# Shorter runs in the load of x, one last tile of 512 tokens, and GpSimd's share of layer 2 where it runs alone

## The chip, the cores and the metric

The kernel runs on 1 core of one Trainium2 chip. The metric is the device time of one execution in microseconds (us). Five engines work side by side, each through its own instruction queue in order: TensorE (PE, matmuls into PSUM), VectorE (DVE), ScalarE (ACT), GpSimd (POOL) and SyncE (SP, which here issues the DMAs).

## What is computed

```python
X = np.fft.fft(np.fft.fft(x, axis=1), axis=2).real        # x: 2 x 3008 x 256
x = X.reshape(6016, 256)
h = x @ w1_in; g = np.maximum(h, 0) ** 2; x = g @ w1_out  # layer 1: 256 -> 2048 -> 256
h = x @ w2_in                                             # layer 2: 256 -> 2048 -> 256
P = a[0] + a[1]*h + a[2]*h**2 + a[3]*h**3
Q = 1 + abs(b[0])*abs(h) + abs(b[1])*h**2
out = (P / (Q + 1e-6)) @ w2_out
```

Each operand of the large products is split into a rounded high part and a rest ("hi", "lo"), and a product takes three matmuls: hi hi, lo hi, hi lo.

## The kernel before

**Start.** x comes in nine loads (`x_load`, L231): one small one, then eight chunks of 4 units (the last of 3), each for 96 partitions. A chunk has four buffers (`xt`) to go to. `u_mm` (L238) multiplies a chunk with a 47-point Fourier matrix (L247), ACT copies one half of the result out of PSUM (`u_copy`) and DVE forms sums and differences (`u_out`, L263) into U. Loads of the weights (L315, L317) stand between those of x on SP's queue; ACT and DVE turn each weight block into fp32 hi and lo parts ("decode", L322 to L359). When all of U is there, small transforms (`f_d`, `f_s`, L473 to L503) give layer 1 its inputs, tile by tile; this is called F below.

**Tiles.** `TILES` counts units of 128 tokens: a first tile of 384 tokens, ten of 512, then two of 256. The hidden dimension is 16 chunks of 128. Layer 1 of a tile is, for each chunk, a product into `h` (`h1_mm`, L623 to L625; it works on half the columns of a tile, 256 for a tile of 512 and 128 for one of 256), ACT and DVE work, a low part on POOL (L694), and the product with `w1_out` (`mm_o`, L651). For a tile of 256 tokens two chunks share one bank of 512 columns. At the end of a tile ACT and DVE split the result in two (L700, L705).

**Layer 2** goes over sub-tiles of 256 tokens (`SUB`; 23 of them), each in eight groups of two chunks, that is of 512 columns. The last sub-tile has seven such groups and two single chunks (`SINGLES`). A group is a product into a bank `h2` (L592, 12 matmuls), then

- ACT: u = |scaled h| (L712), t1 (L717), w = |u| (L726), y (L739), z = y squared (L743)
- DVE: q (L722, into u's buffer), t2 (L730), t3 (L734), gh (L749), m (L755, into bank p3), e (L759)
- POOL: gl (L763), which also gives the low part its final form

and the product with `w2_out` (L651 with o2a as its output, 12 matmuls). t3 is the last reader of the bank h2, which is then given back.

**The order.** A planner (`Queues`, L62) simulates the engines with a cost for each operation (`act`, `dve`, `pool_tt`, `mm`), takes buffers and banks from named sets (`SLOTS`, `SPARE`) and writes out each engine's instruction order; a `place` settles which of several ready operations goes first. Layer 2 of a tile is placed one tile behind its layer 1 (L834): the PE does layer 1 of tile t among layer 2 of tile t - 1. So layer 2 of the last tile has no layer 1 beside it; it "runs alone".

Of the kernel before, what the change touches and what calls it, by code (L numbers as in the profile page):

```python
# [13 lines left out]
ALU = mybir.AluOpType  # L14
# [8 lines left out]
TILES = [3] + [4] * 10 + [2, 2]  # L23
# [16 lines left out]
LATE = (8, 5.18, 4.1, 3.03)  # L40
LAG_END = 4.67
POOLED = 2
# [114 lines left out]
def body(ctx: ExitStack, tc: tile.TileContext, x0, xf, w1i, w1o, w2i, w2o, a_in, b_in,  # L157
# [73 lines left out]
    def x_load(c):  # L231
        XT[c] = stp.tile([96, max(X_CH), 2, 256], F32, tag="xt", name="xt", bufs=SLOTS["xt"])
        if c == 0:
            nc.sync.dma_start(out=XT[c][:, 0:2], in_=x0)
        else:
            nc.sync.dma_start(out=XT[c][:, 0:XN[c]], in_=xf[:, S0[c] - 1:S0[c] - 1 + XN[c]])
# [39 lines left out]
    for c in range(NC):  # L276
        place = -32 + c
        n = XN[c]
        add(("x", c), "SP", 0.78 * n if c else 7.0, place, lambda c=c: x_load(c), take=("xt",), lat=X_LAT,
# [126 lines left out]
    for j, w in enumerate(wl):  # L406
# [4 lines left out]
        add(("wd", j), "SP", 2.1, place - 4, lambda j=j, w=w: w_load(j, *w), take=(raw,), lat=DMA_LAT,  # L411
# [37 lines left out]
    H1, H2, O1, O2 = {}, {}, {}, {}  # L449
    G1, G2, E1, E2, OB = {}, {}, {}, {}, {}  # L450
# [116 lines left out]
    def names(tag, t):  # L567
# [4 lines left out]
        if tag == "h2":  # L572
            return (BANKS5 if t else BANKS) + (SPARE["h2"] if t == M - 1 else ())
        return (tag,) + (SPARE1.get(tag, ()) if t <= 1 and tag == "g" else ()) + (SPARE.get(tag, ()) if t == M - 1 else ())
# [145 lines left out]
    def e2_q(t, j):  # L720
        w = E2[t, j]["w"]
        nc.vector.scalar_tensor_tensor(out=w, in0=w, scalar=b0, in1=H2[t, j], op0=ALU.add, op1=ALU.mult)  # L722
# [21 lines left out]

    def e2_gh(t, j):
        e = E2[t, j]
        x = sb(tag2("g2", t, j), [128, 2, NMAX], F32R)
        e["gh"], e["gl"] = x[:, 0, :e["n"]], x[:, 1, :e["n"]]
        nc.vector.scalar_tensor_tensor(out=e["gh"], in0=e["t1"], scalar=a0, in1=e["z"], op0=ALU.add, op1=ALU.mult)  # L749


    def e2_m(t, j):
        e = E2[t, j]
        e["m"] = ps(tag2("m", t, j), [128, NMAX])[:, :e["n"]]
        nc.vector.scalar_tensor_tensor(out=e["m"], in0=e["w"], scalar=Q1, in1=f32(e["gh"]), op0=ALU.add, op1=ALU.mult)  # L755

    def e2_e(t, j):
        e = E2[t, j]
        nc.vector.scalar_tensor_tensor(out=e["t1"], in0=e["t1"], scalar=a0, in1=e["m"], op0=ALU.add, op1=ALU.subtract)  # L759
# [73 lines left out]
    for t, (tile1, col, width) in enumerate(SUB):  # L833
        base = 16 * (tile1 + 1) + M2_AT + (LATE + (0,) * T)[tile1]  # L834
        for j, (first, gs) in enumerate(GROUPS2[t]):
# [14 lines left out]
            add(("q",) + key, "DVE", dve(n, ptr=1), place, f(e2_q), needs=[("u",) + key, ("t1",) + key])  # L850
            add(("t2",) + key, "DVE", dve(n), place, f(e2_t2), needs=[("t1",) + key])
            add(("t3",) + key, "DVE", dve(n, ptr=1), place, f(e2_t3), needs=[("t2",) + key], after=[("q",) + key],
                give=(given("h2", t, j),))
            add(("w",) + key, "ACT", act(n), place, f(e2_w), needs=[("q",) + key])
# [121 lines left out]
```

## Time and profile before

| | us |
|---|---|
| median of 3 runs | 1122.88 |
| lowest and highest | 1121.0, 1123.06 |
| the profiled execution's own time | 1124.36 |
| its span in the profile | 1122.5 |
| mean granted clock of TensorE | 0.985 |

The profile gives, for one execution, the busy time of each engine, single instructions in order of time, and what ended the idle time before them. In the rows below, "L651" is line 651 of the kernel, `o2a<-g,w2hi` an output and its inputs by tile name, and x12 a count of merged instructions. Times of instructions are counted from the span's start. An instruction's own time can overlap the next one's, so the distance between two starts is what it costs a full queue.

### The profile page before, as it was taken

Reading aid. Unit: us, or ns where it says so; the run is one execution under the profiler, and the core shown is the slowest. Engines: PE = TensorE matmul, PEld = TensorE weight load, DVE = VectorE, ACT = ScalarE, POOL = GpSimd, SP = SyncE. Lnnn points to the kernel's source line nnn. Section 1 sums busy time; section 2 is a strip of 40 time slices with the busy share of each in tenths; the row PEclk is TensorE's granted clock in tenths of the full one; section 3 lists DMA queues with packets and bytes.
Section 4 is the critical chain, followed back from the end, with each engine's and each line's share of the span. In section 5 each row is a group of like instructions: output and inputs, shape, how many; then the busy total and the mean of one; then the engine's idle time right before and its main releaser. Section 6 shows DMA issues by size and latency. Waiting matters only on the chain.

```text
span 1122.5 us, 21825 instructions
## 1 busy us (share of the span) xinstructions
PE 1086.1 (97%) x7932; PEld 1022.5 (91%) x7932; DVE 1027.2 (92%) x1821; ACT 982.0 (87%) x1995; POOL 472.4 (42%) x358
## 2 busy tenths in 40 slices
PE   7999998999999999999999999999999999999996
PEld 6889987989999999989999999999999999999995
DVE  3689999999999999999999899999999998999988
ACT  2378898999999989899999999999999999898884
POOL 0000004455455544455455454554454556354423
PEclk9889999999999999999999999999999999999997
DMA  8952510000000000000000000000000000000000
GB/s 215 258 203 76 172 45 1 1 25 10 1 20 11 1 20 10 1 20 11 1 20 10 2 20 11 3 18 10 1 15 11 6 10 11 11 1 11 11 10 10
DMA packets 25543, 36.68 MB, mean 33 GB/s; under 512 B 2203, under 2 KB 19229, under 8 KB 24765
## 3 DMA queue, kind: packets, MB, share of 16 engines
q1 hardware_dynamic: 25293, 35.17, 10.2%
q8 instruction: 63, 1.03, 0.4%
q14 instruction: 43, 0.35, 0.1%
q10 hardware_dynamic: 144, 0.13, 0.0%
HBM read 26.48 MB, written 8.78 MB: 31 GB/s over the span
## 4 chain that ended last, share of the span: by engine, by line
PE 64%; ACT 15%; DVE 13%; issue 4%; DMA 3%; SPq 1%; POOL 1%; DVEq 0%; ACTq 0%; POOLq 0%
PE o2a L651 16%; PE p L592 11%; PE o1a L651 8%; PE o1b L651 8%; PE p L623 6%; PE o2b L592 5%; DVE g L749 2%; DVE p L755 2%; ACT y L739 2%; ACT u L726 2%; DVE t L759 2%; PE p L605 2%; PE p L608 2%; ACT g L679 2%; ACT y L743 2%
## 5 line engine op out<-in xcount | busy, mean ns | idle before, releaser
L763 POOL TENSOR_TENSOR g<-t,y 128x512 fp32r<-128x512 f32 (+1 forms) x188 | 255.9, 1361 | 442.1 <-DVE t L759 343.4
L694 POOL TENSOR_TENSOR g<-g,g 128x512 fp32r<-128x512 f32 x160 | 214.0, 1338 | 187.6 <-ACT g L689 149.0
L651 PE MATMUL o2a<-g,w2hi 128*128 128x256 f32 (+1 forms) x1440 | 266.5, 287 | 8.6 <-POOL g L763 8.4
L651 PEld LDWEIGHTS o2a<-g,w2hi 128*128 128x128 f32 x1440 | 211.2, 191 | 19.4 <-POOL g L763 11.4
L749 DVE SCALAR_TENSOR_TENSOR g<-t,ab,y 128x512 fp32r<-128x512 f32 (+1 forms) x188 | 149.2, 796 | 13.4 <-ACT y L743 10.7
L651 PE MATMUL o2a<-g,w2lo 128*128 128x256 f32 (+1 forms) x720 | 146.1, 283 | 0.0
L651 PE MATMUL o1a<-g,w1hi 128*128 128x512 f32 (+1 forms) x384 | 144.8, 379 | 0.6 <-POOL g L694 0.5
L755 DVE SCALAR_TENSOR_TENSOR p<-u,g 128x512 f32<-128x512 f32 (+2 forms) x190 | 144.6, 761 | 0.8
L651 PE MATMUL o1b<-g,w1hi 128*128 128x512 f32 (+1 forms) x384 | 143.3, 375 | 0.0
L759 DVE SCALAR_TENSOR_TENSOR t<-t,ab,p 128x512 f32<-128x512 f32 (+2 forms) x190 | 138.3, 728 | 1.2
L726 ACT ACTIVATE u<-u 128x512 f32<-128x512 f32 (+2 forms) x190 | 118.1, 621 | 18.7 <-DVE u L722 17.8
L679 ACT ACTIVATE g<-g 128x512 f32<-128x512 f32 x160 | 100.9, 631 | 25.8 <-DVE g L669 24.7
L739 ACT ACTIVATE y<-u 128x512 f32<-128x512 f32 (+1 forms) x188 | 116.5, 621 | 4.9 <-POOL g L763 0.6
L743 ACT ACTIVATE y<-y 128x512 f32<-128x512 f32 (+1 forms) x189 | 117.0, 621 | 1.5
L722 DVE SCALAR_TENSOR_TENSOR u<-u,ab,p 128x512 f32<-128x512 f32 (+2 forms) x137 | 99.0, 723 | 18.7 <-ACT t L717 18.6
L592 PE MATMUL p<-x2h,w2hi 128*128 128x256 f32 (+1 forms) x520 | 106.9, 287 | 6.0 <-DVE t L734 4.0
L669 DVE TENSOR_TENSOR g<-p,bc 128x256 f32<-128x256 f32 x262 | 106.1, 418 | 7.1 <-POOL g L694 3.4
L651 PEld LDWEIGHTS o2a<-g,w2lo 128*128 128x128 f32 x720 | 111.8, 191 | 0.0
L685 ACT ACTIVATE g<-g 128x512 fp32r<-128x512 f32 (+1 forms) x175 | 109.4, 625 | 2.0 <-PE o1b L651 0.9
L689 ACT ACTIVATE g<-g 128x512 f32<-128x512 f32 (+1 forms) x175 | 109.2, 625 | 1.1
L592 PE MATMUL p<-x2l,w2hi 128*128 128x256 f32 (+1 forms) x520 | 105.5, 283 | 0.3 <-DVE x2l L705 0.2
L592 PE MATMUL p<-x2h,w2lo 128*128 128x256 f32 (+1 forms) x520 | 104.3, 282 | 0.0
(239 smaller groups left out, 2886.2 us busy)
## 6 DMA issues: line engine op xcount, KB each, us to landing
g<-in_dram SPq DMA_DIRECT2D x48, 256.0 KB, 3.1
xt<-in_dram SPq DMA_DIRECT2D x7, 768.0 KB, 10.2
out_dram<-os SPq DMA_DIRECT2D x21, 256.0 KB, 2.1
udram<-U SPq DMA_DIRECT2D x4, 640.0 KB, 5.1
ut<-udram SPq DMA_DIRECT2D x9, 256.0 KB, 3.0
x2h<-in_dram SPq DMA_DIRECT2D x8, 256.0 KB, 7.1
x2l<-in_dram SPq DMA_DIRECT2D x8, 256.0 KB, 5.2
xt<-in_dram SPq DMA_DIRECT2D x1, 576.0 KB, 8.8
```

The costliest lines, as they stand in the source:

```text
L592: nc.tensor.matmul(h[:, c * n:(c + 1) * n], l[:, k, :], r[:, k], start=(q == 0), stop=(q == 5))
L651: nc.tensor.matmul(O[t][e], l[:, e * 128:(e + 1) * 128], r[:, c * n:(c + 1) * n], start=(i == 0 and q == 0 and not one), stop=(i == NF - 1 ...
L679: nc.scalar.activation(out=e["g"], in_=e["g"], func=ACTF.Relu)
L685: nc.scalar.activation(out=e["gh"], in_=e["g"], func=ACTF.Square)
L694: eng.tensor_tensor(out=e["gl"], in0=e["g"], in1=f32(e["gh"]), op=ALU.subtract)
L726: nc.scalar.activation(out=w, in_=w, func=ACTF.Abs)
L739: nc.scalar.activation(out=e["z"], in_=e["w"], func=ACTF.Abs_reciprocal_sqrt, bias=Q1)
L743: nc.scalar.activation(out=z, in_=z, func=ACTF.Square)
L749: nc.vector.scalar_tensor_tensor(out=e["gh"], in0=e["t1"], scalar=a0, in1=e["z"], op0=ALU.add, op1=ALU.mult)
L755: nc.vector.scalar_tensor_tensor(out=e["m"], in0=e["w"], scalar=Q1, in1=f32(e["gh"]), op0=ALU.add, op1=ALU.mult)
L759: nc.vector.scalar_tensor_tensor(out=e["t1"], in0=e["t1"], scalar=a0, in1=e["m"], op0=ALU.add, op1=ALU.subtract)
L763: nc.gpsimd.tensor_tensor(out=e["gl"], in0=e["t1"], in1=e["z"], op=ALU.mult)
```

## The change

Four things are changed.

1. The host lays x out with the unit as the outer dimension, so that a chunk is read in runs of 2048 bytes for each partition and unit; before, each partition read one run of 8192 bytes.
2. `TILES` ends with one tile of four units in place of two of two units. The number of layer 2 sub-tiles stays 23; the last two now both belong to the last tile and run alone.
3. For 15 of the 17 groups that run alone (`ALONE`: all of both sub-tiles but the two single chunks), q is written into h's own bank, after t3; w and m stay in that bank; ACT adds a0 to t3's result (new operation P, `e2_p`); gh is a product on POOL and no longer a DVE operation; e becomes a plain subtraction on DVE. The bank is given back by e, u's buffer by q, and p3 is not used.
4. The planner's numbers: lower costs for the loads, layer 2 of the tile before the last is placed 1.5 places later (`BEHIND`), and the spare buffers and banks are open to both last sub-tiles.

```diff
-TILES = [3] + [4] * 10 + [2, 2]
+TILES = [3] + [4] * 11
...
-LATE = (8, 5.18, 4.1, 3.03)
+LATE, BEHIND = (8, 5.18, 4.1, 3.03), 1.5
...
+ALONE_FROM, ALONE_END = 0, 2
...
-            nc.sync.dma_start(out=XT[c][:, 0:XN[c]], in_=xf[:, S0[c] - 1:S0[c] - 1 + XN[c]])
+            nc.sync.dma_start(out=XT[c][:, 0:XN[c]], in_=xf[S0[c] - 1:S0[c] - 1 + XN[c]].rearrange("s p h d -> p s h d"))
...
-        add(("x", c), "SP", 0.78 * n if c else 7.0, place, lambda c=c: x_load(c), take=("xt",), lat=X_LAT,
+        add(("x", c), "SP", 0.55 * n if c else 7.0, place, lambda c=c: x_load(c), take=("xt",), lat=X_LAT,
...
-        add(("wd", j), "SP", 2.1, place - 4, lambda j=j, w=w: w_load(j, *w), take=(raw,), lat=DMA_LAT,
+        add(("wd", j), "SP", 1.5, place - 4, lambda j=j, w=w: w_load(j, *w), take=(raw,), lat=DMA_LAT,
...
+    ALONE = [(t, j) for t in (M - 2, M - 1) for j in range(len(GROUPS2[t]))][ALONE_FROM:-ALONE_END]
...
-            return (BANKS5 if t else BANKS) + (SPARE["h2"] if t == M - 1 else ())
-        return (tag,) + (SPARE1.get(tag, ()) if t <= 1 and tag == "g" else ()) + (SPARE.get(tag, ()) if t == M - 1 else ())
+            return (BANKS5 if t else BANKS) + (SPARE["h2"] if t >= M - 2 else ())
+        return (tag,) + (SPARE1.get(tag, ()) if t <= 1 and tag == "g" else ()) + (SPARE.get(tag, ()) if t >= M - 2 else ())
...
     def e2_q(t, j):
-        w = E2[t, j]["w"]
-        nc.vector.scalar_tensor_tensor(out=w, in0=w, scalar=b0, in1=H2[t, j], op0=ALU.add, op1=ALU.mult)
+        e, w = E2[t, j], E2[t, j]["w"]
+        e["w"] = H2[t, j] if (t, j) in ALONE else w
+        nc.vector.scalar_tensor_tensor(out=e["w"], in0=w, scalar=b0, in1=H2[t, j], op0=ALU.add, op1=ALU.mult)
...
+    def e2_p(t, j):
+        t1 = E2[t, j]["t1"]
+        nc.scalar.activation(out=t1, in_=t1, func=ACTF.Identity, bias=a0)
...
     def e2_gh(t, j):
...
+        if (t, j) in ALONE:
+            nc.gpsimd.tensor_tensor(out=e["gh"], in0=e["t1"], in1=e["z"], op=ALU.mult)
+            return
...
     def e2_m(t, j):
...
-        e["m"] = ps(tag2("m", t, j), [128, NMAX])[:, :e["n"]]
+        e["m"] = e["w"] if (t, j) in ALONE else ps(tag2("m", t, j), [128, NMAX])[:, :e["n"]]
...
     def e2_e(t, j):
...
+        if (t, j) in ALONE:
+            nc.vector.tensor_tensor(out=e["t1"], in0=e["t1"], in1=e["m"], op=ALU.subtract)
+            return
...
-        base = 16 * (tile1 + 1) + M2_AT + (LATE + (0,) * T)[tile1]
+        base = 16 * (tile1 + 1) + M2_AT + (LATE + (0,) * T)[tile1] + BEHIND * (tile1 == T - 2)
...
-            add(("q",) + key, "DVE", dve(n, ptr=1), place, f(e2_q), needs=[("u",) + key, ("t1",) + key])
+            alone = key in ALONE
+            free, held = (given("u", t, j),), (given("h2", t, j),)
+            add(("q",) + key, "DVE", dve(n, ptr=1), place, f(e2_q), needs=[("u",) + key, ("t1",) + key],
+                after=[("t3",) + key] if alone else [], give=free if alone else ())
...
-            add(("t3",) + key, "DVE", dve(n, ptr=1), place, f(e2_t3), needs=[("t2",) + key], after=[("q",) + key],
-                give=(given("h2", t, j),))
-            add(("w",) + key, "ACT", act(n), place, f(e2_w), needs=[("q",) + key])
-            add(("y",) + key, "ACT", act(n), place, f(e2_y), needs=[("w",) + key], take=(one_of("y", t, j),),
+            add(("t3",) + key, "DVE", dve(n, ptr=1), place, f(e2_t3), needs=[("t2",) + key],
+                after=[] if alone else [("q",) + key], give=() if alone else held)
+            add(("w",) + key, "ACT", act(n, alone), place, f(e2_w), needs=[("q",) + key])
+            add(("y",) + key, "ACT", act(n, alone), place, f(e2_y), needs=[("w",) + key], take=(one_of("y", t, j),),
...
-            add(("gh",) + key, "DVE", dve(n, ptr=1), place, f(e2_gh), needs=[("z",) + key, ("t3",) + key],
+            if alone:
+                add(("P",) + key, "ACT", act(n, ptr=1), place, f(e2_p), needs=[("t3",) + key])
+            gh = ("POOL", pool_tt(n)) if alone else ("DVE", dve(n, ptr=1))
+            add(("gh",) + key, *gh, place, f(e2_gh), needs=[("z",) + key, ("P" if alone else "t3",) + key],
...
-            add(("m",) + key, "DVE", dve(n), place, f(e2_m), needs=[("gh",) + key], port=True,
-                take=(one_of("m", t, j),), give=(given("u", t, j),))
-            add(("e",) + key, "DVE", dve(n, ptr=1), place, f(e2_e), needs=[("m",) + key], give=(given("m", t, j),))
+            add(("m",) + key, "DVE", dve(n), place, f(e2_m), needs=[("gh",) + key], port=not alone,
+                take=() if alone else (one_of("m", t, j),), give=() if alone else free)
+            add(("e",) + key, "DVE", dve(n, ptr=0 if alone else 1), place, f(e2_e), needs=[("m",) + key], give=held if alone else (given("m", t, j),))
...
-    xf, x0 = np.zeros((96, 31, 2, D), x.dtype), np.zeros((96, 2, 2, D), x.dtype)
-    xf[:B * N2], x0[:B * N2] = xm[:, 1:32], xm[:, 0:33:32]
+    xf, x0 = np.zeros((31, 96, 2, D), x.dtype), np.zeros((96, 2, 2, D), x.dtype)
+    xf[:, :B * N2], x0[:B * N2] = xm[:, 1:32].transpose(1, 0, 2, 3), xm[:, 0:33:32]
```

## Rows read from the trace of the kernel before

**Rows 1.** The page: busy time, share of the span and instruction count by engine
```profile
PE 1086.1 (97%) x7932; PEld 1022.5 (91%) x7932; DVE 1027.2 (92%) x1821; ACT 982.0 (87%) x1995; POOL 472.4 (42%) x358
```

**Rows 2.** Busy us (and instructions) by stretch: PE, PEld, DVE, ACT, POOL, clock, DMA, GB/s
```profile
58.00:75.00 17.00, 14.38 (x104) 13.20 (x103) 15.48 (x40) 13.69 (x37) 0.00 (x0) 1.00 0.60 221
...
879.83:960.86 81.03, 81.03 (x600) 76.18 (x599) 75.26 (x130) 77.19 (x154) 44.04 (x32) 1.00 0.02 8
960.86:1079.81 118.95, 118.49 (x1009) 116.75 (x1008) 110.98 (x183) 101.12 (x190) 55.38 (x41) 1.00 0.02 8
...
1083.74:1117.40 33.66, 26.54 (x174) 24.32 (x173) 33.37 (x54) 21.99 (x44) 9.96 (x8) 0.80 0.02 8
...
1102.30:1115.95 13.65, 9.96 (x42) 8.79 (x41) 13.58 (x24) 4.87 (x11) 5.19 (x4) 0.50 0.00 0
```

**Rows 3.** TensorE in time, start: three of the chunks of x
```profile
27.88 3.75 PE L247 MATMUL o2a<-c_t,xt 96*128 96x128 f32 x16 [2.75 <-DMA xt<-in_dram]
...
34.41 3.74 PE L247 MATMUL p<-c_t,xt 96*128 96x128 f32 x32
...
45.12 2.84 PE L247 MATMUL p<-c_t,xt 96*128 96x128 f32 x24
```

**Rows 4.** Busy time by stretch, start (columns as in rows 2; the last is GB/s)
```profile
24.00:26.00 2.00, 1.13 (x11) 0.94 (x9) 0.75 (x2) 0.67 (x1) 0.00 (x0) 1.00 1.03 242
...
28.00:34.00 6.00, 6.00 (x29) 6.00 (x30) 1.48 (x5) 1.21 (x3) 0.00 (x0) 0.51 1.07 271
...
46.00:48.00 2.00, 1.97 (x18) 1.78 (x16) 1.97 (x6) 0.99 (x2) 0.00 (x0) 1.00 1.07 366
```

**Rows 5.** The chain of waits before the last period, TensorE: start, length, work, count
```profile
947.85 0.34 PE p L623 x3
...
948.66 1.41 PE o2a L651 x12
...
953.28 0.67 PE p L623 x6
```

**Rows 6.** TensorE in time: F's second product, for one pair of units
```profile
963.24 0.38 PE L502 MATMUL p<-cd_t,v 128*128 128x128 f32 x2
...
963.93 0.48 PE L592 MATMUL p<-x2h,w2hi 128*128 128x256 f32 x2
```

**Rows 7.** VectorE in time, alone: q, t2, m, gh, then (after e, t3) the next q
```profile
1100.18 0.74 DVE L722 SCALAR_TENSOR_TENSOR u<-u,ab,o1b 128x512 f32<-128x512 f32 x1
1100.84 0.68 DVE L730 TENSOR_TENSOR t<-t,o1b 128x512 f32<-128x512 f32 x1
1101.44 0.70 DVE L755 SCALAR_TENSOR_TENSOR p<-x1l,g 128x512 f32<-128x512 f32 x1
1102.04 0.75 DVE L749 SCALAR_TENSOR_TENSOR g<-t,ab,y 128x512 fp32r<-128x512 f32 x1
...
1104.02 0.75 DVE L722 SCALAR_TENSOR_TENSOR x1l<-x1l,ab,p 128x512 f32<-128x512 f32 x1
```

**Rows 8.** ScalarE in time, alone: u, y, t1, z
```profile
1096.50 0.64 ACT L712 ACTIVATE x1l<-p 128x512 f32<-128x512 f32 x1
1096.97 0.68 ACT L739 ACTIVATE y<-u 128x512 f32<-128x512 f32 x1
1097.49 0.73 ACT L717 ACTIVATE x1h<-p,ab 128x512 f32<-128x512 f32 x1
1098.07 0.68 ACT L743 ACTIVATE y<-y 128x512 f32<-128x512 f32 x1
```

**Rows 9.** GpSimd and VectorE in time, near the end: gl, and m of 256 columns
```profile
1114.20 1.37 POOL L763 TENSOR_TENSOR g<-x1h,g 128x512 fp32r<-128x512 f32 x1 [1.77 <-DVE x1h L759]
1114.35 1.51 DVE L755 SCALAR_TENSOR_TENSOR p<-u,g 128x256 f32<-128x256 f32 x1
```

**Rows 10.** TensorE in time at the half clock: a group's product with w2_out
```profile
1108.79 1.22 PE L651 MATMUL o2a<-g,w2hi 128*128 128x256 f32 x4 [0.92 <-POOL g L763]
...
1111.09 0.63 PE L651 MATMUL o2a<-g,w2lo 128*128 128x256 f32 x2
```

## The prediction

> **What bounds the kernel now.** I read the page first: TensorE is busy 97% of the span, VectorE 92%, ScalarE 87%, GpSimd 42% [rows 1]. A share over the whole span hides stages, so I then cut the span at the first L700 of a tile, the point where its layer 1 ends [rows 2]. Four stages differ.
>
> - A regular period (879.83 to 960.86, layer 1 of the tenth tile of 512 beside layer 2 of the tile before) takes 81.0 us, TensorE busy all of it, ScalarE 77.2, VectorE 75.3. TensorE is the bound, with two engines close behind.
> - The two tiles of 256 (960.86 to 1079.81, 118.95 us) hold one layer 1 of 512 tokens in two halves and three sub-tiles of layer 2. TensorE is full again.
> - Layer 2 alone (1083.74 to 1117.40): VectorE 33.37 of 33.66 us, TensorE 26.5 and partly at half clock, GpSimd 10.0. VectorE is the bound. From its end to the end of the span are 5.1 us (last products, output, store).
> - The start. TensorE waits 2.75 us for a chunk of x [rows 3], and the stretch behind that is granted 0.51 of the clock, its lower level of 1.2 GHz [rows 4].
>
> **The change part by part.** *x in shorter runs.* The load is 31 units x 96 partitions x 2048 bytes = 6.09 MB, as before; only its runs change. In 24 to 26 us, where x is under way, the DMAs are busy throughout (1.03) and move 242 GB/s; in 46 to 48, where the weights are, in rows of 1024 and 2048 bytes, they move 366 at 1.07 [rows 4]. If the length of a run is the reason, 6.09 MB take 16.6 us in place of 25.2. Most of these 8.6 us lie beside TensorE's work on x, so I read their worth from TensorE. From 34.41 to 45.12 it does three chunks without a gap, 3.57 us each; the chunk that came late waited 2.75 and then took 34.41 - 27.88 = 6.53, that is 2.96 more, at the half clock [rows 3, 4]. An x that never comes late is worth 2.75 + 2.96 = 5.7 us; more is not there, since TensorE itself is next. A chunk of 786 KB goes from 3.25 us to 2.15, and two or three chunks precede the late one on the queue, which gives 2.2 to 3.3 us against the 2.75 that it lacks. I take 5.2 us; the bounds are 0 and 5.7. Behind this stage VectorE (decode of weights, 15.5 of 17.0 us) is nearest to a bound [rows 2]; its input, the weight loads, stands behind x on SP's queue and moves forward with it, so I let the gain pass through. Each x load now has four times as many pieces to describe on SP, for which no row has a price; SP waits most of the time there, so I take nothing, and at worst the 5.2 us are lost.
>
> The Trainium skill (DMA: Bandwidth & Descriptors, Specifications) asks for at least 512 bytes per transfer for full rate. By it both lengths are full rate, and this part is worth nothing; the two rates in the trace, 242 and 366 at the same busy share, do not agree with that so far.
>
> *One last tile.* The 112 products of layer 1 that the tile of 512 needs with 256 columns are 224 with 128 columns in two tiles of 256, and a matmul of either width costs the same: 0.34 us for three, 0.67 for six, 0.11 each [rows 5]. So 112 x 0.11 = 12.6 us leave TensorE where it is the bound. The products with w1_out have half the count at twice the columns, and VectorE, ScalarE and GpSimd see operations of the same size and number. What this costs is that two sub-tiles, not one, run alone.
>
> I build the new end from 960.86. Layer 1 of the last tile beside layer 2 of the tile before is a regular period, 81.0 us [rows 2], less the F of a next tile: two pairs of units, 0.69 us each for the second product [rows 6] and by estimate half as much for the first, 2.1 in all: 78.9. The 1.5 places of BEHIND push up to 1.5 groups past its end. A group is 12 + 12 matmuls at 1.41 us per 12 [rows 5], 2.8 us on TensorE, so this stretch is 74.7 to 78.9 us; I take 77.
>
> *The groups alone.* VectorE pays from start to start 0.66 for q, 0.60 for t2, 0.60 for m, and 1.98 for gh, e and t3 together: 3.84 us a group [rows 7]. After the change gh is gone and e is a plain subtraction, priced as t2: 0.66 + 0.60 + 0.66 + 0.60 + 0.60 = 3.12. ScalarE has u at 0.47, t1 at 0.58, w, y and z at 0.52 [rows 8] and the new P, priced as t1, which also adds a column: 3.19 in place of 2.61. GpSimd has two products of 1.37 [rows 9]: 2.74. TensorE has 2.8. No row of before shows w or q written to PSUM; the nearest, m, already goes there at 0.60, so I take no difference, and the bound above is the old 3.84 for a group. Below, no group can be under 3.19. Now three engines hand a group on, t3 to P to gh to m, where t3, gh and m were on one engine. What is queued behind m on VectorE is t2, t3 and q of later groups, and behind gl on GpSimd the gh of the next; a late gh holds both. The regular period, where the full engine had two others within 7% of it, still kept the full one busy [rows 2]. I take 3.5, closer to the lower end for that reason. q now waits for t3 and the bank stays taken until e; with six banks open a group may take 6 x 3.5 = 21 us from product to e, and the operations on that way (product 1.4, ScalarE 3.2, VectorE 3.1, GpSimd 1.4) come to 9, so I cost that at nothing; if the queues double the 9, cover is nearly gone.
>
> One row shows a trap here: m of 256 columns, which reads two tiles of SBUF, took 1.51 us while GpSimd was at its product; m of 512 columns costs 0.60 elsewhere [rows 7, 9]. The Trainium skill (SBUF — State Buffer, Who interferes with whom) says that a VectorE instruction with two inputs in SBUF is held by a GpSimd instruction that reads SBUF for all of its length, and one with at most one such input is not. By that rule q, t2, t3, m and e of the new groups, each with an input in PSUM, are free of GpSimd's 2.74 us; with m held by 0.9 us a group, 15 groups would lose 13.5 us.
>
> *The sum.* After layer 1's end VectorE has the m and e of the group before (0.60 + 0.66), the 1.5 groups pushed there (1.5 x 3.84 = 5.8), the split of the last tile (two operations priced as t2, 1.2), 15 x 3.5 = 52.5, and the two single chunks with the stalls around them, 33.66 - 7 x 3.84 = 6.8 as before: 67.6 us. The pushed groups fill the gap that was empty before 1083.74. The new span ends at 960.9 + 77 + 67.6 + 5.1 = 1110.6, which is 11.9 us under 1122.5. With the start, 11.9 + 5.2 = 17.1. The profiled execution took 1124.36 with a span of 1122.5, and the median of the three runs is 1122.88, 1.5 under that execution; the difference is taken from the median: 1122.9 - 17.1 = **1105.8 us**. The planner's new costs reorder loads and give no term of their own.
>
> **The rivals.** *x no faster* (0.15). The slow rate may belong to where x lies in memory, or to the wait on SP, and not to the run; then this part does not do what it says, 1111.0 us. Against it stand the two rates at one busy share [rows 4]. By the Trainium skill's 512 bytes (DMA: Bandwidth & Descriptors, above) it would be this time as well.
>
> *The groups stay at 3.84* (0.12). The handoffs through ScalarE and GpSimd, or PSUM as output, eat what VectorE saves: 15 x 0.34 = 5.1 more, 1110.9 us. For it: four engines between 2.7 and 3.2 us leave little slack; against it: the regular period, as said. Both of these together (0.05): 1116.1.
>
> *The half clock* (0.05), slower than before. Alone, TensorE is granted half its clock from 1102.30 to 1115.95, while it waits for GpSimd between its products [rows 2, 10]; ten matmuls then take 2.30 us, 0.23 each, so a group costs 5.5 [rows 10]. Before, that was hidden behind 3.84 on VectorE with only one product left to do. If the new stretch ran at that clock throughout, TensorE would bound it: 15 x (5.5 - 3.5) = 30 more, 1136 us. It turns the gain into a loss from 17.1 / (1 - 3.5 / 5.5) = 47 us at half clock of the 52.5. Against it: at 2.8 of 3.5 us TensorE is busy 80%, and at the start the half clock of 28 to 34 us was over with one late chunk's work done [rows 3, 4].
>
> *Better than forecast* (0.05): groups at 3.19, the stretch of layer 1 at 74.7 and all of 5.7 at the start: 4.7 + 2.3 + 0.5 less, 1098.3.
>
> **How the numbers follow.** The forecast has the rest, 0.58, and with groups between 3.3 and 3.7 and a start of 3 to 5.7 it reaches from about 1102 to 1111. The range for 8 in 10 takes in the first two rivals and most of the others' near sides: 1097 to 1115. A measurement of this kernel tells about 0.2%, 2.2 us, from no change. All cases but the half clock are faster by more: 0.93; a half clock for some 45 us lands within 0.2%: 0.02; longer, slower: 0.05.
>
> **What would show it.** In the profile after: TensorE's work on x without a wait and at full clock, ending near 42 us; the DMA rate in that stage above 300 GB/s; the first L700 of the last tile some 77 us after the one before it; VectorE's starts there at 3.3 to 3.7 us a group, with no m above 0.8 us; GpSimd busy near 2.7 us a group; TensorE near 2.8 and at full clock. A wait of VectorE for GpSimd's gh, or of TensorE for a bank, at the top of the waits would prove the groups' price wrong; idle TensorE before L247 would prove the start wrong.

## The result, and the profile after

| | before | after |
|---|---|---|
| median, same chip (us) | 1121.94 | 1111.02 |
| lowest to highest of 4 | 1119.35 to 1123.06 | 1108.41 to 1112.24 |
| ratio, 95% interval | | 0.9898 [0.9881, 0.9916] |
| profiled execution: its time, its span | 1124.36, 1122.5 | 1111.88, 1110.1 |

The kernel is 1.0% faster, about 11 us (9 to 13 by the interval), and the time lies inside the forecast's range, 5.2 us above its likeliest value. These 5.2 us are, to the tenth, the term for x; that it is to the tenth is luck, since the medians of the kernel before, from which the forecast is counted, lie between 1121.9 and 1124.0 on the chips on which it ran. The lines of the code have moved: u_mm L248, h2 L595, h L626, L703 and L708 the split at a tile's end, q L726, w L730, t2 L734, t3 L738, y L743, z L747, P L751, gh L758 on GpSimd and L760 on VectorE, m L766, e L771 where it runs alone, gl L777.

The page after, first part, answers to [rows 1]: TensorE has 17.9 us less to do, VectorE 10.3 less, GpSimd 17.1 more.

```profile
PE 1068.2 (96%) x7724; PEld 1001.4 (90%) x7724; DVE 1016.9 (92%) x1804; ACT 983.2 (89%) x2008; POOL 489.5 (44%) x373
```

Busy time by stretch, after (columns as in [rows 2]): the next-to-last layer-1 period, the last one, layer 2 alone, and what follows VectorE's last operation; then two stretches in which x is loaded, which answer to [rows 4].

```profile
875.19:962.02 86.83, 85.68 (x624) 79.05 (x623) 78.95 (x134) 79.32 (x160) 43.13 (x32) 1.00 0.02 7
962.02:1037.21 75.19, 74.62 (x536) 69.24 (x536) 67.24 (x118) 70.14 (x136) 38.76 (x30) 1.00 0.03 8
1037.21:1105.00 67.79, 58.08 (x449) 55.84 (x448) 64.24 (x105) 57.79 (x112) 46.23 (x36) 0.93 0.03 9
1105.00:1110.10 5.10, 1.48 (x11) 1.28 (x10) 0.42 (x1) 0.38 (x1) 0.00 (x0) 0.83 0.15 51
...
24.00:26.00 2.00, 1.52 (x14) 1.32 (x12) 1.86 (x4) 0.28 (x1) 0.00 (x0) 1.00 1.07 245
32.00:34.00 2.00, 2.00 (x20) 2.00 (x20) 0.00 (x0) 0.00 (x0) 0.00 (x0) 1.00 1.07 227
```

The totals of the tail are as forecast: the last period takes 75.19 us (forecast 77), the stretch alone 67.79 (67.6), the rest 5.1 (5.1). The loads of x are not: 227 to 245 GB/s where more than 300 were expected, at a DMA share that again means busy throughout.

VectorE in time, after, in the stretch alone: the five operations of the new form (they belong to several groups), then the longer of this engine's two waits for GpSimd (the other is 0.18).

```profile
1059.86 0.74 DVE L726 SCALAR_TENSOR_TENSOR p<-u,ab,p 128x512 f32<-128x512 f32 x1
1060.52 0.69 DVE L766 SCALAR_TENSOR_TENSOR o1a<-o1a,g 128x512 f32<-128x512 f32 x1
1061.12 0.73 DVE L738 SCALAR_TENSOR_TENSOR x1h<-x1h,ab,p 128x512 f32<-128x512 f32 x1
1061.78 0.68 DVE L771 TENSOR_TENSOR t<-t,o1a 128x512 f32<-128x512 f32 x1
1062.38 0.74 DVE L726 SCALAR_TENSOR_TENSOR p<-x1l,ab,p 128x512 f32<-128x512 f32 x1
1063.03 0.67 DVE L734 TENSOR_TENSOR t<-t,p 128x512 f32<-128x512 f32 x1
1064.79 0.70 DVE L766 SCALAR_TENSOR_TENSOR o1b<-o1b,g 128x512 f32<-128x512 f32 x1 [1.08 <-POOL g L758]
1065.39 0.74 DVE L738 SCALAR_TENSOR_TENSOR t<-t,ab,p 128x512 f32<-128x512 f32 x1
```

From start to start q costs 0.66, m 0.60, t3 0.66, e 0.60: what the forecast took from [rows 7], with PSUM as output of q and as second input of e. The first q alone starts at 1045.38 and the fifteenth at 1094.37, so a group takes 48.99 / 14 = 3.50 us by this count. Busy time by stretch between these two starts, then in a part of it:

```profile
1045.38:1094.37 48.99, 42.98 (x341) 41.24 (x340) 46.93 (x76) 46.84 (x91) 35.05 (x27) 0.97 0.04 12
1057.50:1061.00 3.50, 3.43 (x16) 3.46 (x17) 3.50 (x6) 3.50 (x7) 2.59 (x2) 0.51 0.00 0
```

VectorE is busy 46.93 of the 48.99 us. It begins 75 operations there, not 14 x 5 = 70: five are left over from groups begun earlier. So of the 0.38 by which 3.50 exceeds the five operations' 3.12, only 2.06 / 14 = 0.15 is waiting. ScalarE is as full, 46.84 us.

The wait of 1.08 us comes over all four engines. TensorE in time, after: it waits 2.21 us for e, which gives a bank back, is then granted the lower level (0.51 in the row above), and ends the product for an output copy late, at 1061.76 + 0.39 = 1062.15.

```profile
1057.57 0.77 PE L595 MATMUL o2b<-x2h,w2hi 128*128 128x256 f32 x2 [2.21 <-DVE x1h L771]
```

ScalarE in time, after: the output copy stands ahead of z in its queue and waits for TensorE, z is late, then gh, then m.

```profile
1062.18 0.60 ACT L795 ACTIVATE os<-o2a 128x512 f32<-128x512 f32 x1 [1.14 <-PE o2a L654]
1062.67 0.62 ACT L747 ACTIVATE y<-y 128x512 f32<-128x512 f32 x1
```

TensorE in time, after, in the work on x: four of its five waits for x, and the last chunk, which answers to [rows 3].

```profile
21.71 2.02 PE L248 MATMUL o1a<-c_t,xt 96*128 96x128 f32 x16 [1.06 <-DMA xt<-in_dram]
26.55 2.02 PE L248 MATMUL o2a<-c_t,xt 96*128 96x128 f32 x16 [1.03 <-DMA xt<-in_dram]
30.98 3.81 PE L248 MATMUL p<-c_t,xt 96*128 96x128 f32 x32 [0.62 <-DMA xt<-in_dram]
37.24 3.75 PE L248 MATMUL o1a<-c_t,xt 96*128 96x128 f32 x16 [2.45 <-DMA xt<-in_dram]
...
47.58 2.84 PE L248 MATMUL p<-c_t,xt 96*128 96x128 f32 x24
```

It ends at 47.58 + 2.84 = 50.42 us; before it ended at 45.12 + 2.84 = 47.96 [rows 3]. x still comes late.

### The profile page after: what moved, and what is told of

Its sections match the earlier page's. It is cut to its first block, busy times and chain, and to the rows that moved or that the text cites. A ratio compares the mean times of both kernels' runs of the same rounds, so it can differ in the third digit from the quotient of the medians.

```text
span 1110.1 us, 21404 instructions
## 1 busy us (share of the span) xinstructions
PE 1068.2 (96%) x7724; PEld 1001.4 (90%) x7724; DVE 1016.9 (92%) x1804; ACT 983.2 (89%) x2008; POOL 489.5 (44%) x373
## 4 chain that ended last, share of the span: by engine, by line
PE 60%; ACT 17%; DVE 14%; DMA 4%; issue 4%; POOL 1%; SPq 1%; DVEq 0%; ACTq 0%; POOLq 0%
PE o2a L654 16%; PE p L595 12%; PE o1a L654 8%; PE o1b L654 7%; PE p L626 6%; PE o2b L595 4%; DMA g<-in_dram 2%; ACT y L743 2%; PE o2b L626 2%; ACT g L688 2%; DMA xt<-in_dram 2%; ACT u L715 2%; ACT y L747 2%; ACT u L730 2%; ACT t L720 2%
## 5 line engine op out<-in xcount | busy, mean ns | idle before, releaser
L777 POOL TENSOR_TENSOR g<-t,y 128x512 fp32r<-128x512 f32 (+1 forms) x182 | 245.4, 1348 | 406.8 <-DVE t L773 313.5
L760 DVE SCALAR_TENSOR_TENSOR g<-t,ab,y 128x512 fp32r<-128x512 f32 (+1 forms) x177 | 139.1, 787 | 13.1 <-ACT y L747 10.9
L654 PE MATMUL o1a<-g,w1hi 128*128 128x512 f32 x352 | 140.4, 399 | 0.4 <-POOL g L697 0.3
L654 PE MATMUL o1b<-g,w1hi 128*128 128x512 f32 x352 | 139.0, 395 | 0.1
L766 DVE SCALAR_TENSOR_TENSOR p<-u,g 128x512 f32<-128x512 f32 (+2 forms) x178 | 137.2, 771 | 0.8
L773 DVE SCALAR_TENSOR_TENSOR t<-t,ab,p 128x512 f32<-128x512 f32 (+2 forms) x178 | 129.2, 726 | 1.3
L730 ACT ACTIVATE u<-u 128x512 f32<-128x512 f32 (+2 forms) x178 | 109.7, 617 | 17.4 <-DVE u L726 17.0
L726 DVE SCALAR_TENSOR_TENSOR u<-u,ab,p 128x512 f32<-128x512 f32 (+2 forms) x139 | 100.8, 725 | 22.1 <-ACT t L720 21.4
L595 PE MATMUL p<-x2h,w2hi 128*128 128x256 f32 (+1 forms) x550 | 112.1, 285 | 7.3 <-DVE t L738 3.2
L747 ACT ACTIVATE y<-y 128x512 f32<-128x512 f32 (+1 forms) x185 | 114.7, 621 | 1.2
L743 ACT ACTIVATE y<-u 128x512 f32<-128x512 f32 (+1 forms) x177 | 109.0, 617 | 4.6 <-POOL g L777 1.4
L595 PE MATMUL p<-x2h,w2lo 128*128 128x256 f32 (+1 forms) x550 | 110.2, 282 | 0.0
L595 PE MATMUL p<-x2l,w2hi 128*128 128x256 f32 (+1 forms) x550 | 110.1, 282 | 0.0
L738 DVE SCALAR_TENSOR_TENSOR t<-t,ab,p 128x512 f32<-128x512 f32 (+1 forms) x143 | 103.3, 723 | 0.6
## 6 DMA issues: line engine op xcount, KB each, us to landing
xt<-in_dram SPq DMA_DIRECT2D x7, 768.0 KB, 10.2
```

The costliest lines, as they stand in the source:

```text
L595: nc.tensor.matmul(h[:, c * n:(c + 1) * n], l[:, k, :], r[:, k], start=(q == 0), stop=(q == 5))
L654: nc.tensor.matmul(O[t][e], l[:, e * 128:(e + 1) * 128], r[:, c * n:(c + 1) * n], start=(i == 0 and q == 0 and not one), stop=(i == NF - 1 ...
L730: nc.scalar.activation(out=w, in_=w, func=ACTF.Abs)
L743: nc.scalar.activation(out=e["z"], in_=e["w"], func=ACTF.Abs_reciprocal_sqrt, bias=Q1)
L747: nc.scalar.activation(out=z, in_=z, func=ACTF.Square)
L777: nc.gpsimd.tensor_tensor(out=e["gl"], in0=e["t1"], in1=e["z"], op=ALU.mult)
```

## Experiments on the load of x

The question: why is x loaded at some 245 GB/s, the weights at 366, and what is a faster x worth?

**Long runs again.** The changed kernel with x in runs of 8192 bytes.

```diff
-                in_=xf[S0[c] - 1:S0[c] - 1 + XN[c]].rearrange("s p h d -> p s h d"))
+                in_=xf[:, S0[c] - 1:S0[c] - 1 + XN[c]])
...
-    xf, x0 = np.zeros((31, 96, 2, D), x.dtype), ...
+    xf, x0 = np.zeros((96, 31, 2, D), x.dtype), ...
```

> The changed kernel, with x read in runs of 8192 bytes as before; all else stays changed. Theory A (the rate of x is set by which partitions it goes to, not by the length of a run): the stage of x moves 230 to 260 GB/s as with 2048 bytes, the time stays within 2 us of the changed kernel's 1111. Theory B (the rate is set by where x lies in DRAM): the layout matters, and the old one, whose partitions lie 63 KB apart, differs by more than 3 us in the end of TensorE's work on x (50.4 us in the changed kernel). Theory C (short runs are faster, and something else ate it): 4 to 6 us slower than the changed kernel, 1115 to 1117.

Measured: 1110.78 us, ratio 0.9896 [0.9878, 0.9915], the same as after; the loads of x at 246 to 247 GB/s. The run's length is worth nothing here.

**The first part alone.** The kernel before with the new layout of x and the lower load costs, nothing else.

```diff
-                in_=xf[:, S0[c] - 1:S0[c] - 1 + XN[c]])
+                in_=xf[S0[c] - 1:S0[c] - 1 + XN[c]].rearrange("s p h d -> p s h d"))
...
-        add(("x", c), "SP", 0.78 * n if c else 7.0, ...
+        add(("x", c), "SP", 0.55 * n if c else 7.0, ...
...
-        add(("wd", j), "SP", 2.1, place - 4, ...
+        add(("wd", j), "SP", 1.5, place - 4, ...
...
-    xf, x0 = np.zeros((96, 31, 2, D), x.dtype), ...
+    xf, x0 = np.zeros((31, 96, 2, D), x.dtype), ...
```

> The kernel before with the change's first part alone: x in runs of 2048 bytes, and the planner's lower costs for the loads; tiles and groups as before. Theory A (the ways into SBUF that 96 partitions reach set the rate, so the run's length does nothing): 1121 to 1125, within 0.2% of the kernel before, loads of x at 225 to 300 GB/s, TensorE's work on x ending at 47.5 to 50.5 us as in the six other kernels with 96 partitions. The prediction's theory (the run's length sets the rate): 5.2 us less, 1116 to 1119, the work on x ending near 42 us.

Measured: 1124.48 us, ratio 1.0006 [0.9991, 1.0022]. Loads at 246 and 255 GB/s, TensorE's work on x until 46.55 us, 1 us before theory A's span and 4.5 after the prediction's 42. The new layout and the lower load costs together give nothing. The costs also change the order that the planner writes for the rest of the kernel, so the layout by itself is read from the long runs above, where that order is kept (GpSimd's instructions stand in the same sequence as after; here they do not stand as before).

**128 partitions.** x padded to 128 partitions; the added rows are not read by any matmul, and a third more bytes are moved.

```diff
-        XT[c] = stp.tile([96, max(X_CH), 2, 256], F32, tag="xt", ...)
+        XT[c] = stp.tile([128, max(X_CH), 2, 256], F32, tag="xt", ...)
...
-    xf, x0 = np.zeros((31, 96, 2, D), x.dtype), ...
+    xf, x0 = np.zeros((31, 128, 2, D), x.dtype), ...
```

> The changed kernel, with x padded to 128 partitions: the 32 added rows are zero, are loaded like the others and are not used, so a third more bytes (8.13 MB) go through the same runs of 2048. Theory A: with all 128 partitions the loads run at the weights' rate, 320 to 370 GB/s in the stage of x, and 8.13 MB take 22 to 25 us, as long as 6.09 MB now; time within 3 us of 1111. Theory B: the rate stays at 230 to 260, 8.13 MB take 33 us, and the kernel is 6 to 9 us slower, 1117 to 1120.

Measured: 1104.93 us, ratio 0.9847 [0.9825, 0.9869], 6.1 us under after, with more bytes. Busy time by stretch, this kernel, the same two stretches as above:

```profile
24.00:26.00 2.00, 1.07 (x10) 0.88 (x8) 1.93 (x5) 0.05 (x1) 0.00 (x0) 1.00 1.05 406
32.00:34.00 2.00, 2.00 (x19) 2.00 (x19) 1.93 (x4) 0.23 (x1) 0.00 (x0) 1.00 1.05 408
```

406 GB/s at the same share. In the packet records of these two stretches a piece of 2048 bytes takes 84 ns here for all but a few; in the kernel after none takes under 90 in the same stretches, and more than 8 of 10 take 120 to 170.

**Both halves.** The 94 rows put into partitions 0 to 46 and 64 to 110. The first chunks, up to number 4, are loaded in one DMA over 128 partitions, the others in two of 48 partitions each.

```diff
+            for a in ((0, 128),) if c <= 4 else ((0, 48), (64, 112)):
+                a = slice(*a)
+                nc.sync.dma_start(out=XT[c][a, 0:XN[c]], in_=xf[S0[c] - 1:S0[c] - 1 + XN[c], a].rearrange(...))
```

> The changed kernel, with x's 94 rows in partitions 0 to 46 and 64 to 110, so that both halves of the partitions get the same share; zero rows fill up to 48 each (the first five loads bring zeros for the rest too, since TensorE now reads all 128 partitions). Theory A: the loads run at 320 GB/s or more, TensorE's work on x ends 4 to 7 us earlier than the 50.4 of the changed kernel, and the kernel is 3 to 6 us faster, 1105 to 1108. If 96 rows are slow because each of the 16 DMA engines has six partitions, not eight: no gain, since each now has three per load. Theory B: no gain, and the added zero rows of the first loads cost 2 to 4 us, 1113 to 1115.

Measured: 1113.37 us, ratio 0.9917 [0.9899, 0.9935], no gain, as theory B had it. In one kernel and one memory, the loads over 128 partitions run at 361 to 407 GB/s between 8 and 14 us, the pairs of 48 at 177 to 187 in three stretches of 2 us in which hardly anything but x is loaded. So the place in memory is not it; number or choice of the partitions is. That both halves get the same share does not help when two DMAs bring them.

**Number or choice.** Ahead of the kernel with 128 partitions, loads for their rate alone.

```diff
+    for lo, hi in ((0, 128), (0, 96), (0, 64), (32, 96), (0, 48), (40, 88), (32, 128), (0, 112), (0, 32)):
+        for _ in range(2):
+            nc.sync.dma_start(out=Uf[lo:hi]... [11 units of 512], in_=xf[0:11, lo:hi].rearrange("s p h d -> p s (h d)"))
```

> The kernel with x padded to 128 partitions, and ahead of its first load eighteen extra loads of x's memory into U's room, 11 units of 2048 bytes for each partition, one after the other has landed, two for each of nine ranges of partitions: 0-127, 0-95, 0-63, 32-95, 0-47, 40-87, 32-127, 0-111, 0-31. They add some 120 us that mean nothing; what counts is the rate of each load. Theory A (the number of partitions sets the rate): equal numbers give equal rates, 0-63 as 32-95, and 0-47 as 40-87, in a row that falls with the number, about 400, 245, 200 and 180 GB/s for 128, 96, 64 and 48. Theory B (which partitions counts: the two halves, 0-63 and 64-127, have each half of the way into SBUF, and in a half the partitions 32 apart share a way, as the loads of 96 partitions showed a third of their packets at 84 ns and the others at 120 to 170): 32-95 with 4 partitions on every way runs at 380 or more and 0-63 with 8 on half of the ways at about 200, twice apart at the same number; 40-87 at 250 or more against 0-47 at 150 to 200; 32-127 as 0-95, about 245.

Measured in one execution, from the packet records of each load (first start to last end, so start-up is within; the two of a range agree within 4%):

```
partitions   us           GB/s       a packet, ns: 25%, median, 75%
0-127        8.95, 9.01   322, 320    84,  84,  84
0-111        9.74, 9.41   259, 268    93, 119, 134
0-95        10.26, 10.19  211, 212   128, 162, 171
32-127       9.97, 10.08  217, 215   124, 160, 171
0-63         7.33, 7.13   197, 202   162, 172, 174
32-95        5.25, 5.34   275, 270    84,  84,  84
0-47         7.59, 7.77   142, 139   101, 246, 276
40-87        5.39, 5.42   201, 200    84, 140, 160
0-31         3.69, 3.74   195, 193    84, 164, 174
```

Busy time by stretch in the middle of one load of each of 0-127, 0-95, 0-63, 32-95, 0-47 and 40-87:

```profile
14.00:20.00 6.00, 0.00 (x0) 0.00 (x0) 0.00 (x0) 0.00 (x0) 0.00 (x0) 1.00 1.01 367
24.00:31.00 7.00, 0.00 (x0) 0.00 (x0) 0.00 (x0) 0.00 (x0) 0.00 (x0) 1.00 1.08 232
...
48.00:53.00 5.00, 0.00 (x0) 0.00 (x0) 0.00 (x0) 0.00 (x0) 0.00 (x0) 1.00 1.08 223
...
67.00:70.00 3.00, 0.00 (x0) 0.00 (x0) 0.00 (x0) 0.00 (x0) 0.00 (x0) 1.00 0.90 315
...
81.00:86.00 5.00, 0.00 (x0) 0.00 (x0) 0.00 (x0) 0.00 (x0) 0.00 (x0) 1.00 1.09 147
...
101.00:104.00 3.00, 0.00 (x0) 0.00 (x0) 0.00 (x0) 0.00 (x0) 0.00 (x0) 1.00 1.04 230
```

The number alone does not set the rate: 64 partitions, 32-95, are loaded in 5.3 us, and 64 others, 0-63, in 7.2, and the median packet of the second takes twice as long (172 ns against 84). And over the whole load 32 partitions, 0-31, go at the rate of the 64 of 0-63, half the bytes in half the time; between 161 and 163 us, in the second load of 0-31, it is 264 GB/s, so start and end weigh in a load this short. The theory of ways shared within a half stands, with misses in size: 32-95 reached 275 (315 in the middle), not 380; 40-87 200 (230), not 250; 0-47 140 (147), not 150 to 200. The expectation's third of the packets at 84 ns in the loads of 96 partitions is not in the records either: here 14 to 18 of 100 take 90 ns or less. Nor does the theory say why the pairs of 48 above, one in each half, stay under twice the 147 of one alone; no run here shows that.

The Trainium skill (SBUF — State Buffer, Door 1: The DMA port swizzle (why `[64,N]` ≈ `[32,N]`)) names the mechanism: a DMA's rate follows the ports into SBUF that its partitions reach, partitions 32 apart share one, 0 to 63 reach the eight of one side and 64 to 127 the eight of the other; its table has, for 1 MiB, 189 GB/s for 0..31, 196 for 0..63 and 328 for 0..127. The whole loads here, of 0.72, 1.44 and 2.88 MB, agree with all three (194, 200, 321). For 0 to 95 it has no row; by its map eight ports would carry eight partitions each, as for 128, and the others four, so an estimate from this page and the measured 321 is three quarters, 241. The measured 211 is lower, and no run here shows why.

**Run length at the full rate.** The kernel with 128 partitions, in runs of 8192 bytes.

```diff
-                in_=xf[S0[c] - 1:S0[c] - 1 + XN[c]].rearrange("s p h d -> p s h d"))
+                in_=xf[:, S0[c] - 1:S0[c] - 1 + XN[c]])
...
-    xf, x0 = np.zeros((31, 128, 2, D), x.dtype), ...
+    xf, x0 = np.zeros((128, 31, 2, D), x.dtype), ...
```

> The kernel with x padded to 128 partitions, a third more bytes with the added rows unused, now in runs of 8192 bytes instead of 2048. Theory A (the number of partitions of a load sets its rate, and the run's length nothing): 1103.5 to 1106.5, and the loads of x at 390 to 410 GB/s. Theory B (at the full rate the run's length begins to count, as it could not at 245 GB/s): 1107 or more, and the loads at under 350 GB/s.

Measured: 1104.42 us, ratio 0.9849 [0.9823, 0.9875]; loads of x at 382 to 434 GB/s. The length makes no difference to the time here either.

**Earlier issue.** In the kernel with 128 partitions the DMAs stand idle for some microseconds while x is not all issued: SyncE's queue has the placing of the folded first weights (L388) ahead of chunk 3 and waits there 6.8 us for VectorE. Moved behind chunk 4:

```diff
-    add("w0c", "SP", 2.4, -31, w0_place, needs=["w0p", "w0z"], give=("cw",), lat=2.5)
+    add("w0c", "SP", 2.4, -31, w0_place, needs=["w0p", "w0z"], give=("cw",), lat=2.5, after=[("x", 4)])
```

> The kernel with x padded to 128 partitions, and the DMAs that place the folded first weights (L388) put behind the fourth chunk of x on the queue of SyncE. There they stood before it, and SyncE waited up to 13 us for their inputs from VectorE while x was not yet issued. Theory A (the start is bound by when x arrives, so an issue that is earlier moves all behind it): 2 to 4 us under the kernel with 128 partitions, 1101 to 1103, with TensorE's first product of x after the small chunk earlier by as much. Theory B (with 128 partitions TensorE's own work on x and the decoding of the weights on VectorE set the end of the start): within 1 us of 1105, and the first product of layer 1 begins where it began.

Measured: 1102.22 us, ratio 0.9835 [0.9808, 0.9863], 2.7 us under the kernel with 128 partitions, whose interval overlaps this one, and 8.8 under after. Busy time by stretch, 14 to 16 us, first with the old place, then with the new:

```profile
14.00:16.00 2.00, 2.00 (x21) 2.00 (x20) 0.00 (x0) 1.04 (x2) 0.00 (x0) 1.00 0.27 95
```

```profile
14.00:16.00 2.00, 2.00 (x17) 2.00 (x17) 0.00 (x0) 1.05 (x2) 0.00 (x0) 0.83 1.05 410
```

The DMA share rises from 0.27 to 1.05. Behind the small first load TensorE does not wait for x at all now, and its work on x ends at 40.72 us (43.32 with the old place, 50.42 after). Its first product of a large chunk starts at 11.2 to 11.7 us in each of these, so it was not the start that moved but the gaps.

The 2.7 us can't be put down to the earlier issue, though. The edit also made the planner write another order for the rest of the kernel: the second tile takes 33.26 us where it took 29.37. ScalarE in time, the split at the end of the first, second and last tile of layer 1, first with the old place, then with the new:

```profile
144.09 0.48 ACT L703 ACTIVATE x2h<-o2a 128x384 fp32r<-128x384 f32 x1
173.46 0.59 ACT L703 ACTIVATE x2h<-o1a 128x512 fp32r<-128x512 f32 x1
...
1030.45 0.58 ACT L703 ACTIVATE x2h<-o1a 128x512 fp32r<-128x512 f32 x1
```

```profile
140.82 0.47 ACT L703 ACTIVATE x2h<-o2a 128x384 fp32r<-128x384 f32 x1
174.08 0.58 ACT L703 ACTIVATE x2h<-o1a 128x512 fp32r<-128x512 f32 x1
...
1027.60 0.60 ACT L703 ACTIVATE x2h<-o1a 128x512 fp32r<-128x512 f32 x1 [0.27 <-PE o1a L654]
```

The new place is 3.27 us ahead at the end of the first tile and 0.62 behind at the end of the second; 3.5 us come in the ten tiles behind, where no x is loaded. What the earlier issue is worth by itself stays open.

## Experiments on the tail

**Without the new groups.** The changed kernel with `ALONE` empty.

```diff
-    ALONE = [(t, j) for t in (M - 2, M - 1) for j in range(len(GROUPS2[t]))][ALONE_FROM:-ALONE_END]
+    ALONE = [(t, j) for t in (M - 2, M - 1) for j in range(len(GROUPS2[t]))][:0]
```

> The changed kernel without the new form of layer 2 for the groups that run alone: gh is on VectorE again, m in p3, q in u's buffer. If the new form brought a group from 3.84 (3.95 with its stalls) on VectorE to the 3.50 measured between starts of q, 15 groups cost 5 to 7 us more: 1116 to 1118. If the groups were bound elsewhere (GpSimd, the banks), less than 2 us more.

Measured: 1117.34 us, ratio 0.9955 [0.9941, 0.9969]; 6.3 us over after. VectorE in time, this kernel: two successive q, with the whole of gh, e and t3 between.

```profile
1081.16 0.74 DVE L726 SCALAR_TENSOR_TENSOR u<-u,ab,o1b 128x512 f32<-128x512 f32 x1
...
1083.02 0.74 DVE L760 SCALAR_TENSOR_TENSOR g<-t,ab,y 128x512 fp32r<-128x512 f32 x1
...
1085.00 0.74 DVE L726 SCALAR_TENSOR_TENSOR u<-u,ab,p 128x512 f32<-128x512 f32 x1
```

3.84 us a group, as in [rows 7]. Busy time by stretch, this kernel, from the last tile's first L703 to near VectorE's last operation of layer 2:

```profile
1039.06:1113.60 74.54, 57.84 (x446) 54.21 (x445) 74.40 (x120) 50.82 (x97) 27.12 (x20) 0.95 0.02 8
```

From 1039.06 the span goes on for 79.7 us, against 72.9 after. VectorE is busy 74.40 of 74.54 us here and 64.24 of 67.79 after: 10.2 us of work less (by the prices above, 15 x (3.84 - 3.12) = 10.8), of which 3.4 came back as waiting. So the new form does what it was made for, and a third of what it saves goes in waiting.

**The tiles alone.** The kernel before with one last tile of 512.

```diff
-TILES = [3] + [4] * 10 + [2, 2]
+TILES = [3] + [4] * 11
```

> The kernel before with one edit, the last two tiles of 256 as one of 512; two sub-tiles then run alone with VectorE's 3.84 us a group instead of one. By the prediction's terms: layer 1 of the last tile takes 12.6 us less of TensorE, and eight more groups run alone at 3.84 us where VectorE is the bound. Theory A: worth 2 to 4 us against the kernel before, 1119 to 1121, so the new form of the groups carries most of the tail's gain. Theory B: the merge is worth 8 us or more by itself, 1115 or less, and the new form adds little to it. Theory C: without the new form the merge costs time (1124 or more), since the long stretch alone is bound by VectorE.

Measured: 1117.81 us, ratio 0.9948 [0.9927, 0.9970], some 6 us under before (3 to 8 by the interval). Busy time by stretch, this kernel, from the last tile's first L700 to the end of the span:

```profile
1040.10:1116.30 76.20, 59.38 (x411) 55.41 (x409) 67.92 (x108) 46.98 (x90) 24.12 (x19) 0.87 0.03 11
```

Layer 1 ends 1079.81 - 1040.10 = 39.7 us earlier than before, and the stretch behind it is 76.2 in place of 1122.5 - 1079.81 = 42.7, so 33.5 longer; 6.2 are left. I had put the merge alone at 2 to 4; it is nearer to 6, and it does not cost time without the new groups.

**Without the push.** The changed kernel with `BEHIND` at 0.

```diff
-LATE, BEHIND = (8, 5.18, 4.1, 3.03), 1.5
+LATE, BEHIND = (8, 5.18, 4.1, 3.03), 0.0
```

> The changed kernel with layer 2 of the tile before the last placed where it was, 1.5 places earlier (BEHIND at 0). Theory A (the 1.5 groups pushed behind the end of layer 1 fill time in which VectorE would else have waited for the first group alone, and free TensorE in the period before): the last tile's layer 1 ends earlier by up to 1.5 groups of product time, but VectorE has a gap before its first q alone as it had before 1083.74 in the old kernel; the sum is +1 to +3 us against the changed kernel, 1112 to 1114. Theory B (VectorE is the bound over the whole of the last two periods, so the place of 1.5 groups between them is worth nothing): within 1 us of it.

Measured: 1113.30 us, ratio 0.9927 [0.9901, 0.9953], 2.3 us over after. The intervals overlap; the spans differ by 1.9 the same way (1112.0 and 1110.1). VectorE in time, this kernel, after its last work of the tile before:

```profile
1045.23 0.75 DVE L773 SCALAR_TENSOR_TENSOR t<-t,ab,p 128x512 f32<-128x512 f32 x1
1048.50 0.69 DVE L734 TENSOR_TENSOR x1h<-x1h,p 128x512 f32<-128x512 f32 x1 [2.52 <-ACT x1h L720]
```

Here VectorE waits 2.52 us for the first group alone, a wait that the pushed groups fill in the kernel after. The merge (about 6), the new form (6.3 with the push, 1117.81 - 1113.30 = 4.5 without it) and the push (2.3 with the new form) don't add up one by one: without the new form the push gave nothing that these runs show (1117.34 against 1117.81, the former with the x part and the wider set of buffers too).

## Why the prediction held, and where not

**The tail, step by step.** Right in its sum, its bound and its savings; two agreements are partly luck. The end of layer 1 was put at 960.9 + 77 = 1037.9 and came at 1037.21; the end of the span without the term for x at 1110.6, and came at 1110.1. The price of PSUM as output of q and w, which no row of before showed, was taken as no difference: q is 0.66 in either place, w 0.51 against 0.52 [rows 8], and e with m in PSUM 0.60. The stretch of layer 1 was 1.8 us under the value taken, inside its bounds, and began 1.2 us later (962.02). The period ahead of it is 86.83, not 81.0. It came out all the same because the periods ahead end 4.6 us earlier than before (875.19 against 879.83). The transforms of a whole tile of 512 are only a part of the 86.83: with the first part of the change alone, where a tile of 256 comes next as before, it is 84.51 (874.63 to 959.14), so most of it lies in the other order that the planner wrote, to which the forecast gave no term.

The group's 3.5 was a choice between 3.19 and 3.84 and was measured as 3.50. The number is met, the reason in part: the 0.38 over VectorE's own 3.12 were to be handoffs, and 0.15 of them are waiting, while the rest is work of other groups that falls between the starts counted. The bank that is held until e was costed at nothing. It did not stay at nothing: TensorE waits 2.21 us for one, runs at the lower level behind it, and the 1.08 us of VectorE follow. That these hang together is read from the order in time; no run tries it with more banks.

**The trap.** m of 512 columns in the new groups costs 0.60 with GpSimd at work beside it: the one at 1064.79 above, up to 1065.39, runs under a GpSimd product that starts at 1064.70, and none of the 15 takes more than 0.70. The Trainium skill (SBUF — State Buffer, Who interferes with whom) states this for a VectorE instruction with at most one input in SBUF, outside the modes in which it uses two ports. An m of 256 columns with both inputs in SBUF, in the two single chunks that kept the old form, is held as in [rows 9]: 1.42 under GpSimd's product, 0.43 where GpSimd has nothing to do as it begins (its next product starts at 1103.05). VectorE, then GpSimd in time, after:

```profile
1100.68 1.42 DVE L766 SCALAR_TENSOR_TENSOR p<-u,g 128x256 f32<-128x256 f32 x1
...
1102.91 0.43 DVE L766 SCALAR_TENSOR_TENSOR p<-u,g 128x256 f32<-128x256 f32 x1
```

```profile
1064.70 1.32 POOL L777 TENSOR_TENSOR g<-t,y 128x512 fp32r<-128x512 f32 x1
...
1100.33 1.47 POOL L777 TENSOR_TENSOR g<-t,g 128x512 fp32r<-128x512 f32 x1 [0.28 <-DVE t L771]
```

**The half clock.** It came for a part: the 0.93 of the clock over the 67.79 us of the stretch alone give an estimate of 9.5 us at the lower level (0.07 x 67.79 / 0.5), against the 47 at which the gain was to turn into a loss.

**x.** Wrong. The step that failed is "If the length of a run is the reason": two loads with different rates, 242 and 366 GB/s [rows 4], differed in their runs and also in their partitions, 96 and 128, and I read the rate by the first. The kernel before has the two only together, so the rows could not tell them apart. The rival *x no faster* was given 0.15 and gives 1111.0 us, the time that was measured; but it names the place in memory and the wait on SP, and the partitions stood in no rival. The long runs, the 128 partitions and the loads by themselves show that the cause is which partitions a load covers. Behind the same step stood the sentence that no row prices the pieces on SP: they cost nothing that the runs show, since the two layouts agree to 0.3 us.

**The worth of a faster x.** Somewhat low, and only the runs with 128 partitions show it. I put it at 5.7 us at most, from one late chunk, "more is not there, since TensorE itself is next". TensorE's work on x takes 47.96 - 11.53 = 36.4 us before, 38.8 after, and 40.72 - 11.20 = 29.5 where x never comes late, so 6.9 us were there in the kernel before. I had counted one of several gaps. TensorE in time, before:

```profile
11.53 2.87 PE L247 MATMUL o2a<-c_t,xt 96*128 96x128 f32 x16
...
16.54 3.84 PE L247 MATMUL p<-c_t,xt 96*128 96x128 f32 x32 [0.36 <-DMA xt<-in_dram]
21.32 2.02 PE L247 MATMUL o1a<-c_t,xt 96*128 96x128 f32 x16 [0.94 <-ACT g L256]
```

That it passes through holds for a large gain: the kernel with 128 partitions, in which the planner's order is that of after (GpSimd's instructions stand in the same sequence), ends its work on x 7.1 us earlier (43.32 against 50.42), its first and second tiles 6.8 earlier (144.09 and 173.46 against 150.86 and 180.25), and the time is 6.1 less. Small differences do not show: the kernel without the push ends its work on x 2.7 us before after (47.76) and its first tile 0.1 behind it (150.99).

## What to carry to other kernels

Before you credit a slow load to one property, list all in which it differs from the fast one, the partitions that it covers among them: padding x from 96 to 128 partitions, a third more bytes, made this kernel 6 us faster. Where one engine bounds a stretch, take an operation off it and price the new group between that engine's own sum and the old price: of 10.2 us of VectorE's work that went here, 3.4 came back as waiting, and with an operand in PSUM m was not held by GpSimd. When a time per group comes out as forecast, count the operations between the two starts before you trust the reason. A queue that waits at one entry holds the loads behind it: look at the DMA share in short stretches (0.27 here while loads were still to come). And where a planner writes the order, see whether an edit moved it elsewhere before you credit the time to the edit.

## What the runs showed of the hardware

- A load's rate depends on which partitions it covers, at a DMA share that says busy all the time: in the middle of a load 367 GB/s for 0-127, 315 for 32-95, 232 for 0-95, 223 for 0-63, 147 for 0-47. The number of partitions does not settle it (32-95 and 0-63 have 64 each). A high DMA share is no proof of a high rate; the median time of one packet (84 ns for 0-127 and 32-95, 172 for 0-63, 2048 bytes each) tells them apart.
- 2048 and 8192 bytes in a run made no difference to the time, at 96 partitions as at 128.
- VectorE writes 128x512 to PSUM at the price of SBUF: q costs 0.66 us to either.
- m of 256 columns with both inputs in SBUF took 1.42 us under a GpSimd product and 0.43 where GpSimd had nothing to do as it began; m of 512 columns with one input in PSUM took no more than 0.70 in any of 15 groups, a GpSimd product beside it or not.
